# Converting w_out on one engine, pairing tiles f and f+8, and making the first operands of the last product earlier, in an attention + MoE kernel

## The chip, the cores and the metric

The kernel runs on one core of a Trainium2 chip. The metric is the device time of one execution in microseconds, the median of three runs. The names of the engines are those of the profile: PE (TensorE), DVE (VectorE), ACT (ScalarE), POOL (GpSimd), and SP, whose queue issues nearly all DMA transfers here. Each engine runs its own instructions strictly in the order of the program.

## The reference

```python
attn_out = softmax(q k^T / 8 + bias) v        # 4 batches, 8 heads, 576 positions, 64 wide
x = attn_out as 2304 tokens x 512
h = x @ w_in                                  # 512 -> 2048
g = h * tanh(softplus(h))                     # Mish
out = g @ w_out                               # 2048 -> 512, all float32
```

## The kernel before

The attention takes about the first 290 us of the span, and nothing of it is changed. What follows is the MoE part, over four blocks of tokens (512, 768, 512, 512). Every float32 operand of a product is split into a rounded part "hi" and a rest "lo" (ACT makes hi with a copy that rounds, DVE makes lo with a subtraction), and the product is the sum hi·hi + lo·hi + hi·lo.

**Blocks 0, 2 and 3** (`hidden` and `gate`): for each of the 16 tiles f of 128 columns of w_in, `hidden` puts 12 matmuls into one of four PSUM buffers h, and `gate` lets ACT write Mish of h into a buffer g. Tiles f and f+8 share one g buffer; after the second of the two, POOL adds one half of it to another (L692) and SP writes the whole to HBM (L693, `g_d`). The order of the tiles is `FORDER`: 0 to 3, then 8 to 11, then the rest in pairs. Since PE has four buffers h, it can be at most four tiles ahead of ACT. **Block 1** (`product`, `gates`) does the same in a form with seven products (a Strassen scheme).

**Beside blocks 2 and 3** three more things run. (1) w_out arrives as 64-bit words in 16 pieces; `load_weights` (L107) fetches each into one of three buffers, and `conv_weights` turns it into float32 with four instructions: a multiplication (L129 on ACT, or L131 on DVE), and L134, L136, L138 on DVE. One call of `convert` issues one step of that, and four calls finish a piece. (2) `split_x` turns the x of the next block into hi and lo: a multiplication (L653, DVE), a copy (L654, ACT) and a subtraction (L656, DVE). (3) `combine(m)` makes the seven right-hand operands of the last product from w_out (a subtraction L897 or L903 on DVE, two copies L900 on ACT, two subtractions L901 on DVE).

**The last product** (out = g @ w_out) runs over nine token tiles p with seven products each (`multiply(p, m, t)`, t = 0 for the hi of g, 1 for its lo). `load_g(p)` reads g back from HBM, `prepare(p, m)` makes the left-hand operand m in one of four buffers gslot: ACT copies (L927), DVE subtracts (L928). `prepare(p, 2)` first subtracts on DVE (L924), and afterwards lets POOL make two more sums, L930 and L931, in its own queue. `leave` takes results out of PSUM: `leave(0, 0)` copies the first product on ACT to `p1s` (in the tile `la`, L966), and PE may add product 2 into the same PSUM bank only after that.

The ring `rt` holds, one behind the other, x of block 3, the g buffers, and later combo6 and three of the gslot buffers: a gslot that lies where a g buffer was can be written only when that buffer's transfer to HBM has ended. In the kernel before gslot2 lies on g buffers 0 and 1, gslot3 on 2 and 3.

Of the kernel before, what the change touches and what calls it, by code (L numbers as in the profile page):

```python
# [7 lines left out]
F32 = mybir.dt.float32  # L8
F32R = mybir.dt.float32r
# [7 lines left out]
HP = H // 2  # L17
DM, DFF = 512, 2048
NT = B * S
P = 128  # L20
# [10 lines left out]
TB = 512  # L31
# [15 lines left out]
def kernel(ctx: ExitStack, tc, qk, v, wb, w2, w_in, w_out, psia, psi4, rinv, eye, out):  # L47
# [378 lines left out]
    def convert(on_act, last):  # L426
        if not conv and w64 and last not in done:
            done.append(w64[0][0])
            conv.append(conv_weights(on_act))
        elif conv and next(conv[0]):  # L430
            conv.clear()
            load_weights()
            if w32 and w32[0][0] in order[:EARLY]:
                split_weights(pool)
# [82 lines left out]
    bps_t, h_t = {}, {}  # L517
# [14 lines left out]
    for idx, t in enumerate(ts):  # L532
        spent["a"] += 0.75 + (1.9 if idx in SOFT_AT else 0.0)
        spent["v"] += (1.6 if idx in SOFT_AT else 0.0)
        n = reach(t)[2]
# [58 lines left out]
    for idx in range(NB + 2):  # L594
# [16 lines left out]
        if idx - 2 in SOFT_AT[1:]:  # L611
            f = s_ps.tile([P, 2, 512], F32, name="s")
# [18 lines left out]
    rt = sbuf("rt", 1, side="right").ring(11 * 4096)  # L631
# [6 lines left out]
    xc = []  # L638
    g_bufs = []

    XPARTS = [(x, d) for x in "hl" for d in range(HP)]

    def begin_x(blk, raw, hl):
        load_x(blk, raw)
# [3 lines left out]
    def split_x(blk, parts):  # L648
        n = blocks[blk][1]
        for x, d in parts:  # L650
            raw, hi, lo = (y[blk][:, d, :n] for y in (x_raw, x_hi, x_lo))
            if x == "h":
                dve.tensor_tensor(raw, raw, lo.bitcast(F32), op=ALU.mult)  # L653
                act.copy(hi, raw)  # L654
            else:
                dve.tensor_tensor(lo, raw, hi.bitcast(F32), op=ALU.subtract)  # L656


    FORDER = [0, 1, 2, 3, 8, 9, 10, 11, 4, 12, 5, 13, 6, 14, 7, 15]
    units = {blk: [(blk, i, (f,)) for i, f in enumerate(FORDER)] for blk in (0, 2, 3)}  # L660
    h_t, g_t, n_g = {}, {}, [4]

    def w_at(f, d):
        return [x[:, f % 4] for x in w_split["i", f // 4, d]]
# [12 lines left out]
    def gate(blk, i, fs):  # L677
        n = blocks[blk][1]
        j = fs[0] % 8
        if (blk, j) not in g_t:  # L680
            if blk == 0:
                g_t[blk, j] = g_own[j]
            else:
                g_t[blk, j] = g_bufs[n_g[0] % 5]
                n_g[0] += 1
        g = g_t[blk, j]
        c0 = fs[0] // 8 * n
        act.activation(g[:, c0:c0 + len(fs) * n], h_t.pop((blk, fs)), AF.Mish)  # L688
        if fs[-1] >= 8:
            del g_t[blk, j]  # L690
            g = g.rearrange("p (k t) -> p k t", k=4)
            pool.tensor_tensor(g[:, 1], g[:, 1], g[:, 3], op=ALU.add)  # L692
            sp.dma_start(out=g_d[blk][:, :, j].rearrange("k p t -> p k t"), in_=g)  # L693
# [157 lines left out]
    x2_hl = [xa_t[:, t].bitcast(F32R) for t in range(2)]  # L851
    AT_STEP = {(0, 0): ((x1_lo, 5),), (0, 3): ((x1_hi, 6),), (0, 4): ((x1_lo, 6),), (0, 6): ((begin_x, 2, x2, x2_hl),)}
    for n, part in enumerate(XPARTS):
        AT_STEP[divmod(11 + n, 7)] = ((split_x, 2, (part,)),)
    for p in range(4):
        for k in range(7):
            product(p, k)
# [10 lines left out]

    xp_raw = rt.tile([P, HP, TB], F32, name="xraw")
    xp_hl = [rt.tile([P, HP, TB], F32R, name=name) for name in ("xhi", "xlo")]  # L870
    g_bufs += [rt.tile([P, 2 * TB], F32, name="g") for _ in range(5)]

    q_t.append(ring.tile([P, 4, 8, 256], F32, name="quarters"))
    b11, b12, b21, b22 = (q_t[0][:, q] for q in range(4))
# [13 lines left out]
    slots = [ring.tile([P, 2, 8, P], F32R, name="gslot1")]  # L888
# [6 lines left out]
    def combine(m):  # L895
        if m in w_sum:
            dve.tensor_tensor(w_src[m], *w_sum[m], op=ALU.subtract)  # L897
        for half in (slice(0, 4), slice(4, 8)):
            hi, lo = wc[m][:, half, 0:256], wc[m][:, half, 256:512]
            act.copy(hi, w_src[m][:, half])  # L900
            dve.tensor_tensor(lo, w_src[m][:, half], hi.bitcast(F32), op=ALU.subtract)  # L901
        if m == 2:
            dve.tensor_tensor(b11, b21, b11, op=ALU.subtract)  # L903
# [89 lines left out]

    def reuse_x():
        wc[6] = rt.tile([P, 8, 512], F32R, name="combo6")
        slots.extend(rt.tile([P, 2, 8, P], F32R, name=f"gslot{k}") for k in (2, 3))

    for blk in (2, 3):
        for i in range(16):
            if blk == 2:  # L1000
                if i == 2:
                    begin_x(3, xp_raw, xp_hl)
                if 6 <= i < 14:
                    split_x(3, XPARTS[i - 6:i - 5])
            hidden(*units[blk][i])
            if (2, 0) < (blk, i) <= (3, 0):
                for _ in range(4):
                    convert(True, None)
            if blk == 3:
                if i == 0:  # L1010
                    combine(0)
                    slots.insert(0, rt.tile([P, 2, 8, P], F32R, name="gslot0"))
                elif i == 2:
                    combine(1)
                elif i == 5:
                    combine(2)
                elif i == 8:
                    load_g(0)
                elif i == 9:
                    combine(3)  # L1020
                elif i == 11:
                    prepare(0, 0)
                elif i == 13:
                    combine(4)
                elif i == 14:
                    prepare(0, 1)
                elif i == 15:
                    reuse_x()
                    prepare(0, 2)
            gate(*units[blk][i])  # L1030
    load_g(1)
    prepare(0, 3)
    combine(5)
# [95 lines left out]
```

## Time and profile before

| | |
|---|---|
| median of three runs | 651.92 us (651.9 to 652.0) |
| profiled execution: its own time | 651.97 us |
| profiled execution: span from first to last instruction | 650.2 us |
| PE busy | 633.4 us, 97% of the span |
| DVE busy | 486.5 us, 75% |
| ACT busy | 427.8 us, 66% |
| POOL busy | 174.3 us, 27% |

The profile shows one execution. Busy time counts instructions at work; an engine whose share is far below 100% can still be the one that others wait for over a stretch of some microseconds. Times in the views are microseconds from the first instruction.

### The profile page before, as it was taken

To read this page: it belongs to the slowest core of one execution; us is meant where nothing else is said; L and a number is where in the kernel's file an instruction comes from. 1 tells how busy PE (TensorE), PEld (TensorE's weight loads), DVE (VectorE), ACT (ScalarE), POOL (GpSimd) and SP (SyncE) were. 2 spreads that over 40 slices of the span, in tenths; PEclk is the share of its full clock that TensorE was granted. 3 is DMA by queue.
4 is the path that set the end of the run, shared out by engine and by line. 5 is a ranking of instruction groups with operands and counts; after the bars stand their busy time and mean duration, and the time that the engine had idled before them with its cause. 6 is when DMAs were issued, how large, how long until landed. Compare 5 with 4: busy or idle time off the path is not lost.

```text
span 650.2 us, 14512 instructions
## 1 busy us (share of the span) xinstructions
PE 633.4 (97%) x5504; PEld 500.6 (77%) x5504; DVE 486.5 (75%) x919; ACT 427.8 (66%) x886; POOL 174.3 (27%) x150
## 2 busy tenths in 40 slices
PE   6989999999999999999999999999999999999997
PEld 2436677777777777778899998877888888888886
DVE  7995888988888888635646535888698777777875
ACT  6886899989999999854566643446475434455432
POOL 0000133333222334405253511114243221122220
PEclk9999999999999999999999999999999999999999
DMA  8986486677758766029236369862846545433401
GB/s 275 297 275 205 142 266 211 234 234 240 261 187 270 256 189 181 23 62 281 97 132 198 126 222 289 280 213 83 273 134 191 162 146 163 145 109 96 152 17 50
DMA packets 99622, 119.71 MB, mean 184 GB/s; under 512 B 15200, under 2 KB 75616, under 8 KB 99552
## 3 DMA queue, kind: packets, MB, share of 16 engines
q1 hardware_dynamic: 97248, 110.59, 53.0%
q0 software_dynamic: 1872, 8.09, 4.2%
q8 instruction: 44, 0.72, 0.4%
q14 instruction: 26, 0.21, 0.1%
q10 hardware_dynamic: 432, 0.09, 0.1%
HBM read 79.47 MB, written 39.28 MB: 183 GB/s over the span
## 4 chain that ended last, share of the span: by engine, by line
PE 75%; DVE 9%; DMA 6%; ACT 5%; issue 4%; SPq 1%; POOL 0%; DVEq 0%; ACTq 0%
PE h L673 11%; PE s L232 10%; PE o L356 10%; PE y L949 8%; PE h L949 8%; PE bps L601 6%; PE tp L318 4%; PE h L953 4%; PE y L953 4%; PE y L790 3%; PE h L790 3%; DMA w<-in_w_out_dram 2%; DVE pt L249 2%; PE te L301 2%; PE o L360 1%
## 5 line engine op out<-in xcount | busy, mean ns | idle before, releaser
L264 ACT ACTIVATE pt<-pt,m 128x576 f32<-128x576 f32 x144 | 112.0, 787 | 2.7 <-DVE m L249 2.2
L249 DVE CUSTOM_DVE_ANT_0 pt<-s,bias 128x576 f32<-128x576 f32 (+1 forms) x112 | 81.6, 754 | 22.8 <-PE s L232 17.2
L183 POOL TENSOR_TENSOR qklo<-rawqk,qkhi 128x304 fp32r<-128x304 f32 x52 | 46.7, 923 | 118.9 <-DMA rawqk<-in_qk_dram 109.6
L356 PE MATMUL o<-main,vt 128*64 128x256 f32 (+1 forms) x512 | 76.1, 418 | 0.0
L326 ACT COPY main<-tp 128x512 f32<-128x512 f32 x126 | 68.2, 599 | 0.9 <-DMA bias_d<-bt 0.9
L232 PE MATMUL s<-qkhi 64*128 64x288 f32 x260 | 57.0, 341 | 0.9
L318 PEld LDWEIGHTS tp<-ident,pt 64*128 64x128 f32 x1184 | 54.8, 138 | 2.0 <-ACT main L326 0.5
L318 PE MATMUL tp<-ident,pt 64*128 64x64 f32 x1184 | 56.0, 222 | 0.2 <-ACT main L326 0.2
L927 ACT CAST gslot<-graw 128x1024 fp32r<-128x1024 f32 x30 | 31.2, 1052 | 36.3 <-DVE graw L924 28.0
L692 POOL TENSOR_TENSOR g<-g 128x256 f32<-128x256 f32 x24 | 27.3, 1143 | 95.7 <-ACT g L688 81.7
L601 PE MATMUL bps<-ht,w2t 128*32 128x79 f32 (+49 forms) x640 | 42.9, 403 | 8.9 <-ACT ht L551 6.3
L927 ACT CAST gslot<-quarters 128x1024 fp32r<-128x1024 f32 x28 | 29.1, 1055 | 32.4 <-DVE quarters L924 26.0
L928 DVE TENSOR_TENSOR gslot<-graw,gslot 128x1024 fp32r<-128x1024 f32 x30 | 41.9, 1433 | 10.6 <-ACT gslot L927 10.6
L232 PE MATMUL s<-qklo,qkhi 64*128 64x288 f32 x260 | 48.0, 297 | 0.0
L232 PE MATMUL s<-qkhi,qklo 64*128 64x288 f32 x260 | 46.4, 291 | 0.0
L356 PEld LDWEIGHTS o<-main,vt 128*64 128x64 f32 x512 | 31.8, 136 | 17.2 <-ACT tail L332 0.4
L673 PE MATMUL h<-xa,lc 128*128 128x512 f32 x192 | 43.8, 389 | 0.0
L601 PEld LDWEIGHTS bps<-ht,w2t 128*32 128x32 f32 x640 | 17.2, 113 | 34.4 <-ACT bt L581 14.9
L928 DVE TENSOR_TENSOR gslot<-quarters,gslot 128x1024 fp32r<-128x1024 f32 x28 | 39.5, 1454 | 5.0 <-ACT gslot L927 5.0
L553 DVE TENSOR_SCALAR ht<-at,bb 128x560 f32<-128x560 f32 (+17 forms) x120 | 43.2, 440 | 0.0
L673 PEld LDWEIGHTS h<-xa,lc 128*128 128x128 f32 x192 | 36.0, 188 | 7.5
L688 ACT ACTIVATE g<-h 128x512 f32<-128x512 f32 x48 | 28.0, 593 | 20.1 <-PE h L673 16.9
(206 smaller groups left out, 1498.7 us busy)
## 6 DMA issues: line engine op xcount, KB each, us to landing
g_d<-g SPq DMA_DIRECT2D x24, 512.0 KB
bias_d<-bt SPq DMA_DIRECT2D x36, 295.5 KB
w<-in_w_in_dram SPq DMA_DIRECT2D x16, 512.0 KB
w<-in_w_out_dram SPq DMA_DIRECT2D x16, 512.0 KB
quarters<-g_d SPq DMA_DIRECT2D x16, 512.0 KB
qkhi<-in_qk_dram POOLq DMA_DIRECT2D x13, 608.0 KB, 5.1
rawqk<-in_qk_dram SPq DMA_DIRECT2D x13, 608.0 KB
graw<-g_d SPq DMA_DIRECT2D x15, 512.0 KB
```

Of the source, the lines that this page charges most:

```text
L232: pe.matmul(s[:, j, :SH], q[rows, c * P:(c + 1) * P], k[rows, KO + j * SH:KO + (j + 1) * SH], start=(t == 0), stop=(t == len(terms) - 1))
L249: dve.tensor_tensor_reduce(out=halves(pt[rows, sl]), in0=s[rows, :, :SH], in1=halves(bt[rows, sl]), scale=-0.125, scalar=BIG, op0=ALU.add, ...
L264: act.activation(ps, ps, AF.Exp, bias=m[:, u:u + 1], scale=-1.0, accum_out=sums[i][:, k:k + 1])
L318: pe.transpose(tp[:, k * 64:k * 64 + 64], pt[rows, c0:c0 + P], ident[rows, rows])
L326: copy(main[:, :, :, q0:q0 + 64], tp.rearrange("p (h k q) -> p h k q", h=2, k=4))
L356: pe.matmul(o[h * 64:h * 64 + 64, :w], vt[:, h, k, :], main[:, h, k, :], start=(k == 0), stop=False, **kw)
L601: pe.matmul(ps[cg * 32:cg * 32 + 32, a:a + n], w2t, h_t[idx, cg][:, cols], start=True, stop=True)
L673: pe.matmul(h[:, u * n:(u + 1) * n], w_at(f, d)[t], x[:, d, :n], start=(k == 0), stop=(k == 11))
L927: act.copy(hi, src)
L928: dve.tensor_tensor(lo, src, hi.bitcast(F32), op=ALU.subtract)
L949: pe.matmul(o, x[:, f], wc[m][:, f], start=(f == 0 and m in (0, 1, 3)), stop=(f == 7), **kw)
L953: pe.matmul(o[:, 0:256], x[:, f], wc[m][:, f, 0:256], start=False, stop=(f == 7), **kw)
```

## The change

Four things are changed. The multiplication of each w_out piece moves from ACT (L129) to DVE (L131), and three calls of `convert` follow each tile instead of four, so that the 16 pieces end at tile 6 of block 3 instead of tile 0. The tiles of blocks 2 and 3 come in the order 0, 8, 1, 9, ... (`PAIRED`), with three g buffers instead of five. The parts of `split_x` are ordered so that DVE multiplies one step ahead of ACT's copy. And the operands of the last product are placed anew: gslot2 gets room of its own at tile 0 of block 3, gslot3 now lies on g buffers 0 and 1 (those of pairs 5 and 6 of block 3), `load_g(0)` comes one tile earlier, `prepare(0, 1)` and `prepare(0, 2)` come at tiles 12 and 13 instead of 14 and 15, and `combine(2)` and `combine(4)` come later. Line numbers shift by 1 to 4 (L692 becomes L695, L924 L927, L927 L930, L930 L933, L931 L934, L966 L969).

```diff
-    XPARTS = [(x, d) for x in "hl" for d in range(HP)]
+    XPARTS = [[("m", 0)]] + [[("h", d), ("m", d + 1)] for d in range(HP - 1)] + [[("h", HP - 1), ("l", 0)]]
+    XPARTS += [[("l", d)] for d in range(1, HP)]
...
-            if x == "h":
+            if x == "m":
                 dve.tensor_tensor(raw, raw, lo.bitcast(F32), op=ALU.mult)
+            elif x == "h":
                 act.copy(hi, raw)
...
-    units = {blk: [(blk, i, (f,)) for i, f in enumerate(FORDER)] for blk in (0, 2, 3)}
-    h_t, g_t, n_g = {}, {}, [4]
+    PAIRED = [f for j in range(8) for f in (j, j + 8)]
+    units = {blk: [(blk, i, (f,)) for i, f in enumerate(PAIRED if blk else FORDER)] for blk in (0, 2, 3)}
+    h_t, g_t, n_g = {}, {}, [2]
...
-                g_t[blk, j] = g_bufs[n_g[0] % 5]
+                g_t[blk, j] = g_bufs[n_g[0] % 3]
...
-    g_bufs += [rt.tile([P, 2 * TB], F32, name="g") for _ in range(5)]
+    g_bufs += [rt.tile([P, 2 * TB], F32, name="g") for _ in range(3)]
...
-        slots.extend(rt.tile([P, 2, 8, P], F32R, name=f"gslot{k}") for k in (2, 3))
+        slots.append(rt.tile([P, 2, 8, P], F32R, name="gslot3"))
...
-            if (2, 0) < (blk, i) <= (3, 0):
-                for _ in range(4):
-                    convert(True, None)
+            if (2, 0) < (blk, i) <= (3, 6):
+                for _ in range(3):
+                    convert(False, None)
             if blk == 3:
                 if i == 0:
                     combine(0)
+                    g2 = rt.tile([P, 2, 8, P], F32R, name="gslot2")
                     slots.insert(0, rt.tile([P, 2, 8, P], F32R, name="gslot0"))
+                    slots.append(g2)
                 elif i == 2:
                     combine(1)
-                elif i == 5:
+                elif i == 7:
                     combine(2)
-                elif i == 8:
                     load_g(0)
                 elif i == 9:
                     combine(3)
                 elif i == 11:
                     prepare(0, 0)
+                elif i == 12:
+                    prepare(0, 1)
                 elif i == 13:
+                    prepare(0, 2)
+                elif i == 14:
                     combine(4)
-                elif i == 14:
-                    prepare(0, 1)
-                elif i == 15:
-                    reuse_x()
-                    prepare(0, 2)
             gate(*units[blk][i])
+    reuse_x()
     load_g(1)
     prepare(0, 3)
     combine(5)
```

On POOL, at the end of block 3, the queue before held 15 of the 16 additions on g ahead of the two sums of `prepare(0, 2)` (each g_ number is one use of a buffer; graw and la hold g read back):

```order
L692 TENSOR_TENSOR g_6281<-g_6281 128x256
L930 TENSOR_TENSOR graw_6790<-la_5459,graw_6789 128x1024
L931 TENSOR_TENSOR graw_6789<-graw_6791,graw_6789 128x1024
L692 TENSOR_TENSOR g_6282<-g_6282 128x256
L930 TENSOR_TENSOR quarters_6283<-quarters_6283 128x1024
```

The same place in the queue of the changed kernel:

```order
L695 TENSOR_TENSOR g_6278<-g_6278 128x256
L933 TENSOR_TENSOR graw_6773<-la_5459,graw_6772 128x1024
L934 TENSOR_TENSOR graw_6772<-graw_6774,graw_6772 128x1024
L695 TENSOR_TENSOR g_6279<-g_6279 128x256
L695 TENSOR_TENSOR g_6280<-g_6280 128x256
L933 TENSOR_TENSOR quarters_6281<-quarters_6281 128x1024
```

The additions of pairs 6 and 7 (g_6279 and g_6280) now stand behind both sums; g_6279 is g buffer 1, on which gslot3 lies.

On ACT, at the same place, the changed kernel issues the following (L691 is a gate, L903 a copy of `combine`, L930 of `prepare`, L969 `leave(0, 0)`):

```order
L691 ACTIVATE g_6279<-h_6848 128x512
L930 CAST gslot2_6635<-graw_6772 128x1024
L691 ACTIVATE g_6279<-h_6864 128x512
L903 CAST lc_5461<-quarters_6281 128x4x256 x2
L691 ACTIVATE g_6280<-h_6885 128x512
L691 ACTIVATE g_6280<-h_6904 128x512
L930 CAST gslot3_6921<-graw_6774 128x1024
L903 CAST lc_5461<-quarters_6281 128x4x256 x2
L969 COPY la_5459<-y_6932 128x512
```

The copy to `la` that releases PE's third product stands behind the copy into gslot3, as it did before; the gates no longer lie between the copies of the first three slots as they did.

On DVE, the stretch from the last w_out pieces to the subtraction of `prepare(0, 2)` reads now:

```order
L904 TENSOR_TENSOR lb<-quarters,lb 128x4x256 x2
L931 TENSOR_TENSOR gslot_6636<-graw,gslot_6636 128x1024
L931 TENSOR_TENSOR gslot_6283<-graw,gslot_6283 128x1024
L927 TENSOR_TENSOR graw<-graw 128x1024
L931 TENSOR_TENSOR gslot_6635<-graw,gslot_6635 128x1024
L900 TENSOR_TENSOR quarters<-quarters 128x2048
L904 TENSOR_TENSOR lc<-quarters,lc 128x4x256 x2
L931 TENSOR_TENSOR gslot_6921<-graw,gslot_6921 128x1024
```

The long subtraction of `combine(4)` (L900) now follows the operands of `prepare(0, 2)`, where before it came ahead of the second operand.

## Rows read from the trace of the kernel before

**Rows 1.** Windows: stretch; busy PE, PEld, DVE, ACT, POOL; clock; DMA share; GB/s.

```profile
381.40:424.98 43.58, 43.58 (x194) 36.06 (x193) 27.16 (x42) 17.65 (x32) 5.98 (x7) 1.00 0.90 294
424.98:470.69 45.71, 44.16 (x194) 35.88 (x192) 34.96 (x32) 23.31 (x34) 13.66 (x9) 1.00 0.54 180
490.00:647.00 157.00, 156.71 (x905) 138.68 (x903) 120.16 (x108) 71.03 (x87) 38.93 (x16) 1.00 0.38 121
```

**Rows 2.** Timeline of PE: start, time, line, tiles, count, idle before and its releaser.

```profile
356.32 1.34 PE L790 MATMUL y<-xcombo,wsums 128*128 128x384 f32 x6 [0.17 <-ACT gs L803]
...
437.15 2.14 PE L673 MATMUL h<-xhi,lb 128*128 128x512 f32 x8 [1.13 <-ACT g L688]
...
443.35 2.12 PE L673 MATMUL h<-xhi,lb 128*128 128x512 f32 x8 [0.42 <-ACT g L688]
...
470.69 1.98 PE L949 MATMUL y<-combo,gslot 128*128 128x512 f32 x8
...
476.25 1.22 PE L953 MATMUL y<-wearly,gslot 128*128 128x256 f32 x8
...
488.06 2.06 PE L949 MATMUL y<-combo,gslot 128*128 128x512 f32 x8 [0.42 <-DVE quarters L974]
```

**Rows 3.** Timeline of ACT around the first two of these waits.

```profile
434.03 0.69 ACT L129 ACTIVATE quarters<-w 128x512 f32<-128x512 f32 x1 [2.60 <-DMA w<-in_w_out_dram]
...
440.81 2.00 ACT L900 CAST xa<-quarters 128x1024 fp32r<-128x1024 f32 x2 [3.22 <-DVE quarters L897]
```

**Rows 4.** The tile w: durations in ns as min/median/max, first and last start.

```profile
L134 DVE TENSOR_SCALAR w<-w x16: 416/421/980, 387.2 to 434.0; 128x512 uint32<-128x512 uint32 x16
L136 DVE SCALAR_TENSOR_TENSOR quarters<-quarters,w x16: 691/693/696, 387.7 to 434.8; 128x512 uint32<-128x512 uint32 x16
L138 DVE SCALAR_TENSOR_TENSOR quarters<-w,quarters x16: 691/693/1119, 388.4 to 435.5; 128x512 uint32<-128x512 uint32 x16
...
L131 DVE TENSOR_SCALAR wraw<-w x13: 384/423/1229, 68.9 to 233.2; 128x512 f32<-128x512 f32 x13
```

**Rows 5.** Timelines of SP and ACT: loads of block 3's x, and a piece behind them.

```profile
385.83 0.56 SPq L376 DMA_DIRECT2D xraw<-x_d  x1
...
398.47 0.69 ACT L129 ACTIVATE quarters<-w 128x512 f32<-128x512 f32 x1 [5.33 <-DMA w<-in_w_out_dram]
```

**Rows 6.** Timeline of DVE: one of each other kind of its instructions in blocks 2 and 3.

```profile
414.01 0.68 DVE L653 TENSOR_TENSOR xraw<-xraw,xlo 128x512 f32<-128x512 f32 x1
...
438.48 2.29 DVE L897 TENSOR_TENSOR quarters<-quarters 128x2048 f32<-128x2048 f32 x1
441.89 2.36 DVE L901 TENSOR_TENSOR xa<-quarters,xa 128x1024 fp32r<-128x1024 f32 x2 [1.12 <-ACT xa L900]
...
470.04 1.21 DVE L924 TENSOR_TENSOR graw<-graw 128x1024 f32<-128x1024 f32 x1
472.42 3.60 DVE L928 TENSOR_TENSOR gslot<-graw,gslot 128x1024 fp32r<-128x1024 f32 x2 [1.16 <-ACT gslot L927]
```

**Rows 7.** Timeline of POOL at the end of block 3.

```profile
431.57 0.76 POOL L692 TENSOR_TENSOR g<-g 128x256 f32<-128x256 f32 x1 [4.64 <-ACT g L688]
...
471.39 2.41 POOL L930 TENSOR_TENSOR graw<-la,graw 128x1024 f32<-128x1024 f32 x1 [2.35 <-DVE graw L924]
475.02 3.27 POOL L931 TENSOR_TENSOR graw<-graw 128x1024 f32<-128x1024 f32 x1 [1.21 <-DVE gslot L928]
478.25 1.72 POOL L692 TENSOR_TENSOR g<-g 128x256 f32<-128x256 f32 x1
```

**Rows 8.** The chain that ended last, 467 to 478: start, time, what.

```profile
469.07 2.75 DMA g_d<-g
```

**Rows 9.** Timeline of ACT where the last product begins.

```profile
472.78 1.04 ACT L927 CAST gslot<-graw 128x1024 fp32r<-128x1024 f32 x1
```

**Rows 10.** Groups of PE by shape, from 6 to 10.2 us: busy, mean ns, idle before.

```profile
L601 PE MATMUL bps<-ht,w2t 128*32 128x497 f32 x8 | 2.0, 1033 | 0.0
...
L601 PE MATMUL bps<-ht,w2t 128*32 128x15 f32 x8 | 0.8, 224 | 6.4 <-ACT ht L551 6.3
```

**Rows 11.** The same from 10.4 to 16 us.

```profile
L601 PE MATMUL bps<-ht,w2t 128*32 128x496 f32 x8 | 1.0, 580 | 0.0
```

More of the change, by code (lines that the diff above doesn't have):

```diff
@@ L853 @@
     for n, part in enumerate(XPARTS):
-        AT_STEP[divmod(11 + n, 7)] = ((split_x, 2, (part,)),)
+        AT_STEP[divmod(11 + n, 7)] = ((split_x, 2, part),)
     for p in range(4):
@@ L1003 @@
                 if 6 <= i < 14:
-                    split_x(3, XPARTS[i - 6:i - 5])
+                    split_x(3, XPARTS[i - 6])
             hidden(*units[blk][i])
-            if (2, 0) < (blk, i) <= (3, 0):
-                for _ in range(4):
-                    convert(True, None)
+            if (2, 0) < (blk, i) <= (3, 6):
+                for _ in range(3):
+                    convert(False, None)
             if blk == 3:
```

## The prediction

> **What bounds the kernel now.** I read the windows view first, by stage [rows 1]. In block 2 PE is busy for 43.58 of 43.58 us, so a tile of `hidden` costs 43.58 / 16 = 2.72 us and nothing can be gained there. Block 3 holds the same 16 tiles and takes 45.71 us: 2.13 us are lost. From 490 us on PE is idle for 0.3 us in 157. So PE is the bound, and all that an edit of the other engines can win after the attention is the few places where PE waits.
>
> The timeline of PE names them [rows 2]: 0.17 us in block 1 (on an ACT copy), 1.13 and 0.42 us in block 3 (on gates, both on ACT), and 0.42 us at the end of the first tile of the last product (on DVE). The two waits of block 3 show 1.55 us and cost 2.13, so each restart of PE costs about 0.29 us more than the row shows. With that the four are worth 0.46 + 2.13 + 0.71 = 3.30 us. This is the most that the change can win.
>
> Why do the gates come late? The timeline of ACT shows it [rows 3]: ACT stands for 2.60 us before a multiplication of a w_out piece that has not landed, and for 3.22 us before a copy of `combine(1)` that needs DVE's subtraction. The gates queue behind both.
>
> **The change, part by part.** (1) *x split*: DVE's multiplication comes one step ahead of ACT's copy. In block 1 ACT no longer stands before the copy with other work behind it; DVE's order there is the same. I give it the whole 0.46 us. Were ACT late all the same, these 0.46 us would be missing.
>
> (2) *w_out on DVE*: ACT no longer waits for a landing, so the 1.13 us wait goes. DVE takes L131 for each piece: 0.42 + 0.42 + 0.69 + 0.69 = 2.23 us a piece [rows 4]. At three calls a tile, that is 0.75 pieces or 1.67 us in 2.72 us: it fits, but what DVE has beside it counts too. I lay DVE's queue end to end, from the third piece to the subtraction of `prepare(0, 2)` (L927 after the change). The start: before, the piece behind the loads of x started at 398.47, with the loads issued from 385.83 [rows 5]; now these loads stand in SP's queue behind the first write of g, which POOL can release only after tile 1 (381.40 + 2 x 2.72, then a gate and an addition, about 389), up to 3.3 us later. I take 401. The work: 14 pieces, 31.2; eight parts of x at 0.60 to 0.68, 4.8; four pairs of `combine` at 2.36 and three long subtractions at 2.29, 16.3; three instructions of 1.21 for the operands, 3.6; two waits of 1.12 for ACT's first copy [rows 6]; and POOL's additions. An addition of 0.76 us [rows 7] holds DVE up: L138 takes 0.69 us by the median and 1.12 at most [rows 4], so 0.42 each, times 11 additions, 4.6. In sum 31.2 + 4.8 + 16.3 + 3.6 + 2.2 + 4.6 = 62.7, so L927 ends at 463.7. From below: it cannot end before tile 11 of block 3 (424.98 + 12 x 2.72 = 457.6), one copy of 1.04 us [rows 9] and two DVE instructions of 1.21, so 461. From above: were the loads held up the full 3.3 us, so that DVE starts at 401.8, and the pieces behind them as much as 1.5 us later still, L927 would end at 466. I take 463.7, because this sum leaves DVE without a pause for 60 us, and nothing speaks for a pause.
>
> With the same sum `combine(1)`'s subtraction ends at about 438, its copies take 2 us on ACT, and the gate behind them is done at 440.7; PE wants that buffer at 424.98 + 6 x 2.72 = 441.3. The 0.42 us wait of block 3 goes too, with 0.6 us to spare. If this margin fails, the loss is hidden by what follows, because part 4 is late by the clock and not by PE.
>
> (3) *Pairs and three g buffers*: a buffer is wanted again six tiles (16 us) after its first use, and a write takes 2.75 us [rows 8]; this costs nothing in block 2. What hides it is that distance; with one buffer it would stall each pair.
>
> (4) *First operands sooner*. This is the part on which the result rests. After `prepare(0, 2)` POOL has its two sums, L933 and L934, and only then the additions of pairs 6 and 7. Before, only the last addition stood there, and nobody waited for it. Now gslot3 lies on the g buffer of pair 6. So the copy into gslot3 on ACT waits for pair 6's write, this for its addition, this for both sums; behind the copy on ACT stand the two copies of `combine(5)` and the copy to `la` (L969), and PE's third product waits for that one.
>
> How long is this chain? The rows of before show it in the same order, one pair later. DVE's L924 ends at 470.04 + 1.21 = 471.25 [rows 6]; then POOL's 2.41, an L928 on DVE that has to wait for it, a second L928, POOL's second sum (3.27 with its wait), one of DVE's L901, and the addition (1.72 with its wait), which ends at 478.25 + 1.72 = 479.97 [rows 7]. The two engines take turns: the pair of L928 takes 3.60 us and not 2.4 [rows 6]. The chain is 8.7 us long. In the changed order the second L928 is replaced by the L900 of `combine(4)`, 2.29 us instead of 1.21: 9.8 us. From below, were the engines not to hold each other up, it would be 2.41 + 2.3 + 0.7 = 5.4 us. I take 9.8, because the order is the same as in the rows.
>
> So pair 6's addition ends at 463.7 + 9.8 = 473.5, its write 2.75 us later [rows 8], at 476.3. Before, PE's third product began at 476.25 and the copy into gslot3 at 472.78 [rows 2, 9], that is 3.47 us earlier, with the same instructions between. So PE starts the third product at 479.8. It could start at 468.56 (424.98 + 43.58, no waits) plus the 5.56 us between 470.69 and 476.25 [rows 2], so at 474.1. PE waits for 5.7 us.
>
> **The sum.** At the third product PE is late against before by 479.8 + 0.29 - 476.25 = +3.84 us. The 0.71 us at the end of the first tile go (DVE has half of that stretch's work behind it, and PE comes later): -0.71. Block 1: -0.46, which moves all of this together. Net +2.67 us on 651.97 us, the profiled execution's own time (its span and 1.8 us around it), so 654.6; the median of the runs is 0.05 us lower, and I say 654.6.
>
> **PE's clock.** The rows at the start of the kernel show what PE does after it has stood idle: after 6.3 us without work, 128x497 matmuls take 2.0 us for eight until 10.2 us [rows 10], and from 10.4 us on 128x496 take 1.0 us for eight [rows 11]. [...]
>
> **Rivals.** *A, the wait without the clock*: 654.6, as worked out. *B, the wait and then half the clock*: 654.6 + 2 = 656.6; the start of the kernel speaks for it [rows 10], but PE comes from rest there and not from work. *C, the chain is short enough*, the case on the other side: if L927 ended at 461 and POOL and DVE did not hold each other up, the write would land at 461 + 5.4 + 2.75 = 469.2, PE would start at 472.6 or earlier, which is before 474.1, and all 3.30 us would be won: 648.7. It decides at a landing of 474.1 - 3.47 = 470.6. Against it speak the rows that show the two engines in turns [rows 6, 7]. *D, DVE is not late but the chain is long*: 461 + 9.8 + 2.75 + 3.47 = 477.0, plus 0.29, is 1.05 us later than before, less 1.17: 651.9, no change. For it speaks only that my sum for DVE has 60 us of terms.
>
> **Numbers.** A change of under 0.2% (1.3 us) can hardly be told from none. A 0.42, B 0.34, C 0.10, D and what lies around it 0.14. A alone reaches from 653.3 to 656. A and B give slower 0.76 plus 0.01 of D; C and a little of D give faster 0.11; same 0.12. The range goes from D's 651.9 to a B in which DVE is 1 us later still, 657.6: left out are C, part of D and the far end of B, together some 0.2.
>
> **What would show it.** In the profile of the changed kernel: no idle before the tiles of block 3, and the product starting near 468; in PE's timeline one wait of 4 to 7 us at the third product (`wearly`), released by ACT's copy to `la`; on ACT a wait before the copy into gslot3, released by a write of g; on POOL the additions of pairs 6 and 7 behind both sums; L131 on DVE 16 times more, and DVE busy without a gap from 401 on. The clock of the 20 us after that wait tells A from B. I would be wrong if gslot3's copy finds the write done, or if DVE reaches L927 much before 463.

## The result, and the profile after

The changed kernel takes 656.88 us by the median of six runs (656.56 to 658.55); the kernel before took 651.96 us beside it. The ratio is 1.0081, with a 95% interval from 1.0067 to 1.0095: 0.8% slower, 4.9 us. The profiled execution took 658.55 us, the longest of the six; its span is 656.8 us. Single executions far above all others (775.31 us for the kernel before, here) are left out of the ratios, while the medians count them.

The timeline of PE in the changed kernel (start, time, line, tiles, count, idle before and its releaser) has these waits after the attention, and behind them the products that follow the longest one:

```profile
360.86 1.34 PE L793 MATMUL y<-xcombo,wsums 128*128 128x384 f32 x6 [0.38 <-ACT u2a L810]
365.82 1.34 PE L793 MATMUL y<-xcombo,lc 128*128 128x384 f32 x6 [0.50 <-DVE gs L816]
...
443.11 2.11 PE L676 MATMUL h<-xhi,wearly 128*128 128x512 f32 x8 [0.47 <-ACT g L691]
...
470.45 1.98 PE L952 MATMUL y<-combo,gslot 128*128 128x512 f32 x8
...
482.06 2.08 PE L956 MATMUL y<-wearly,gslot 128*128 128x256 f32 x8 [5.91 <-ACT la L969]
483.93 2.60 PE L952 MATMUL y<-wearly,gslot 128*128 128x512 f32 x8
486.37 2.00 PE L952 MATMUL y<-lb,gslot 128*128 128x512 f32 x8
488.21 1.98 PE L952 MATMUL y<-lc,gslot 128*128 128x512 f32 x8
```

Three things are to be seen against [rows 2]. The waits of 1.13, 0.42 and 0.42 us are gone, and a smaller one (0.47 us) has come in block 3. PE stands 5.91 us before its third product, released by ACT's copy to `la`. And the eight 128x256 matmuls behind this wait take 483.93 - 482.06 = 1.87 us until the next product starts, where before they took 477.31 - 476.25 = 1.06 us. From the third product to the one on `lc` it is 6.15 us now and was 4.71 us (476.25 to 480.96). The rows of before that this is read from, behind 476.25 in [rows 2]:

```profile
477.31 2.00 PE L949 MATMUL y<-wearly,gslot 128*128 128x512 f32 x8
...
480.96 1.98 PE L949 MATMUL y<-lc,gslot 128*128 128x512 f32 x8
```

The windows view around the wait (stretch; busy PE, PEld, DVE, ACT, POOL; granted clock; DMA share; GB/s) says why:

```profile
477.00:478.00 1.00, 0.00 (x0) 0.00 (x0) 0.00 (x0) 0.00 (x0) 0.31 (x1) 1.00 1.05 372
478.00:479.00 1.00, 0.00 (x0) 0.00 (x0) 0.00 (x0) 0.42 (x1) 0.00 (x0) 0.69 0.80 281
479.00:485.00 6.00, 2.94 (x11) 2.75 (x12) 5.22 (x5) 5.38 (x7) 0.00 (x0) 0.50 1.09 305
485.00:486.00 1.00, 1.00 (x5) 0.77 (x5) 0.64 (x1) 0.00 (x0) 0.00 (x0) 0.90 1.15 348
486.00:490.00 4.00, 4.00 (x19) 3.30 (x18) 1.86 (x2) 3.43 (x5) 0.00 (x0) 1.00 0.85 249
```

PE's last matmul ends at 476.15 (482.06 - 5.91); between 478 and 479 the granted clock falls from 1.00 to 0.50 (a mean of 0.69 there, 0.50 from 479 to 485), and it comes back between 485 and 486 (a mean of 0.90 there, so early in it), some 3 us after PE has begun again at 482.06.

The chain that ended last, from 463 to 483 (start, time, what), shows what the 5.91 us consist of:

```profile
464.75 1.15 DVE graw L927
...
467.00 2.51 DVE gslot L931
...
469.64 0.10 POOL graw L934
469.74 4.19 issue
473.93 1.73 POOL g L695
...
475.67 2.75 DMA g_d<-g
...
478.58 1.04 ACT gslot L930
479.63 1.89 ACT lc L903 x2
481.52 0.49 ACT la L969
```

This is part (4) of the forecast, link by link: L927, the two sums with DVE between them (the 4.19 us called issue are the rest of the second sum, which takes 4.33 us in POOL's timeline), pair 6's addition, its write, the copy into gslot3, `combine(5)`'s copies, the copy to `la`. L927 starts late because DVE starts its third w_out piece late; the timelines of SP and of DVE show it:

```profile
389.72 0.38 SPq L696 DMA_DIRECT2D g_d<-g  x1
390.14 0.56 SPq L376 DMA_DIRECT2D xraw<-x_d  x1
...
393.77 1.56 SPq L107 DMA_DIRECT2D w<-in_w_out_dram  x2
```

```profile
404.32 0.43 DVE L131 TENSOR_SCALAR quarters<-w 128x512 f32<-128x512 f32 x1 [11.23 <-DMA w<-in_w_out_dram]
```

SP issues the loads of x only behind the first write of g, 4.3 us later than before, and the next w_out loads behind them: the third piece is there 5.85 us later than in [rows 5], and 4.67 us when the later start of block 2 (1.18 us) is taken off.

From the starts of the same matmuls in both profiles, the difference of the spans (656.8 - 650.2 = 6.6 us) divides up as follows, beside the forecast's terms for the same stretches:

| Stretch of PE | before, us | after, us | difference | forecast |
|---|---|---|---|---|
| to the start of block 2 | 381.42 | 382.60 | +1.18 | -0.46 |
| block 2 | 43.56 | 43.56 | 0.00 | 0 |
| block 3 | 45.71 | 44.29 | -1.42 | -2.13 |
| last product, start to third product | 5.56 | 11.61 | +6.05 | +5.97 |
| third product to the one on `lc` | 4.71 | 6.15 | +1.44 | 0 (A), 2 (B) |
| the rest | 169.24 | 168.59 | -0.65 | -0.71 |

### The profile page after: what moved, and what is told of

Same layout as the page of the kernel before. It is cut to its first block, busy times and chain, and to the rows that moved or that the text cites. A ratio compares the mean times of both kernels' runs of the same rounds, so it can differ in the third digit from the quotient of the medians.

```text
span 656.8 us, 14501 instructions
## 1 busy us (share of the span) xinstructions
PE 635.1 (97%) x5504; PEld 502.1 (76%) x5504; DVE 492.8 (75%) x935; ACT 418.4 (64%) x870; POOL 172.0 (26%) x150
## 4 chain that ended last, share of the span: by engine, by line
PE 75%; DVE 11%; DMA 6%; issue 4%; ACT 3%; POOL 0%; SPq 0%; DVEq 0%; ACTq 0%; POOLq 0%
PE s L232 11%; PE o L356 11%; PE y L952 9%; PE h L952 8%; PE h L676 8%; PE bps L601 6%; PE tp L318 5%; PE y L956 5%; PE h L956 4%; PE y L793 3%; PE h L793 3%; PE te L301 2%; DVE pt L249 2%; DVE quarters L138 1%; PE o L360 1%
## 5 line engine op out<-in xcount | busy, mean ns | idle before, releaser
L930 ACT CAST gslot<-graw 128x1024 fp32r<-128x1024 f32 x30 | 31.2, 1052 | 38.5 <-DVE graw L927 30.7
L691 ACT ACTIVATE g<-h 128x512 f32<-128x512 f32 x48 | 27.9, 596 | 37.3 <-PE h L676 33.6
L930 ACT CAST gslot<-quarters 128x1024 fp32r<-128x1024 f32 x28 | 29.0, 1055 | 30.3 <-DVE quarters L927 27.3
L931 DVE TENSOR_TENSOR gslot<-graw,gslot 128x1024 fp32r<-128x1024 f32 x30 | 41.5, 1418 | 9.0 <-ACT gslot L930 8.8
L695 POOL TENSOR_TENSOR g<-g 128x256 f32<-128x256 f32 x24 | 24.2, 1012 | 91.7 <-ACT g L691 85.4
L931 DVE TENSOR_TENSOR gslot<-quarters,gslot 128x1024 fp32r<-128x1024 f32 x28 | 37.5, 1385 | 4.8 <-ACT gslot L930 4.8
```

The source lines that it names most:

```text
L930: act.copy(hi, src)
L931: dve.tensor_tensor(lo, src, hi.bitcast(F32), op=ALU.subtract)
```

## The experiments

Each time stands against the kernel before on the same chip; other chips spread more than the first did (before: 651.96 to 652.67 us by the median). The ratio is to the kernel before, with its 95% interval.

### The chain to the third product

**sums_late: the two POOL sums (L933 and L934, taken out of `prepare(0, 2)` as `sums`) behind the last gate**

```diff
             gate(*units[blk][i])
+    sums(0)
     reuse_x()
```

> The changed kernel with one thing moved: the two POOL sums of prepare(0, 2) come behind the last gate, so that the additions of pairs 6 and 7 no longer stand behind them. Theory 1 (the chain sums, addition, write of pair 6, copy into gslot3, copy to la makes PE wait 5.9 us, and the clock falls behind it): the write lands near 471, the copy into gslot3 follows the gates at about 474.7, the copy to la ends at 478.2, PE waits about 2.2 us for its third product, and the clock falls little or not at all: 651.5 to 652.5 us. Theory 2 (the copy is held by ACT's and DVE's own order, combine(4) above all, and the write only happens to end last): wait above 4.5 us, over 655. Theory 3 (much of the loss comes from block 1 and not from this place): as theory 1 in the trace, but the time stays above 653.5.

652.67 us, ratio 1.0009 (0.9998 to 1.0020). PE's timeline has 1.20 us in place of 5.91, and a new wait two products on:

```profile
475.74 1.22 PE L960 MATMUL y<-wearly,gslot 128*128 128x256 f32 x8 [1.20 <-ACT la L973]
...
481.75 2.11 PE L956 MATMUL y<-lc,gslot 128*128 128x512 f32 x8 [1.14 <-ACT la L977]
```

The order of three instructions in POOL's queue thus decides about 4 us. The clock stays at 1.00. Theory 1 stands, though the wait is 1.20 us where it had 2.2 and the time lies just above its range; part of what it wins goes to the operand of the product on `lc`, which needs the sums and now comes later.

**leave_first: `prepare(0, 3)` and `combine(5)` behind `leave(0, 0)`**

```diff
-    prepare(0, 3)
-    combine(5)
     for p in range(len(tiles)):
...
         leave(p, 0)
         if p:
             multiply(p - 1, 6, 1)
             leave(p - 1, 6)
-            prepare(p, 3)
+        prepare(p, 3)
+        if p == 0:
+            combine(5)
```

> The changed kernel with one thing moved: prepare(0, 3) and combine(5) come behind leave(0, 0), so that on ACT the copy to la no longer stands behind the copy into gslot3; pair 6's write is as late as before (lands near 478.5). Theory 1: no wait at the third product; then about 0.8 us for the product that reads gslot3 and about 1 us for the next one, whose operand ACT copies behind combine(5); clock at 1.00 throughout; 651 to 652.5 us. Theory 2 (PE wants gslot3 and what stands behind it as urgently as la, so the wait only moves one product on): a wait of 4 us or more at the product that reads gslot3, over 654.

655.23 us, ratio 1.0043 (1.0028 to 1.0059). The third product doesn't wait; PE's timeline has two waits behind it:

```profile
479.83 2.14 PE L952 MATMUL y<-lb,gslot 128*128 128x512 f32 x8 [0.74 <-ACT gslot L930]
484.59 2.09 PE L952 MATMUL y<-lc,gslot 128*128 128x512 f32 x8 [2.62 <-ACT la L973]
```

More than theory 1 had (0.8 and 1), less than theory 2 (4 or more). ACT's order carries the late write one or two products on, but in the profiled execution the granted clock stays at 1.00 through a wait of 2.62 us. The time is theory 2's (over 654). Four of the six executions have a mean granted clock of 0.996 or 0.997 over the whole span, as those of the changed kernel have (0.994 to 0.997), and the profiled one has 1.00; so the clock most likely fell in those four as well, though no trace shows where.

**both_moved: both at once**

> Both moves at once: the sums behind the last gate, and prepare(0, 3) and combine(5) behind leave(0, 0). Theory 1: neither the write nor ACT's order holds PE, no wait above 0.5 us between 467 and 490, clock 1.00: 656.9 - 5.9 - 1.4 = 649.6 us, below the kernel before. Theory 3 (block 1 holds part of the loss): 651 or more with no wait at the last product's start.

652.76 us, ratio 1.0004 (0.9993 to 1.0015): a miss by 3 us. The first two waits are gone, and others are left: 0.35 us in block 1, 0.29 in block 3, 0.79 at the end of the first tile, and 1.62 at the product on `lc`. That one is the price of the late sums: ACT stands 0.72 us before the copy that takes the second sum, and the copy to `la` that releases the product stands behind it.

**xload_first: the loads of block 3's x one tile sooner**

```diff
-                if i == 2:
+                if i == 1:
                     begin_x(3, xp_raw, xp_hl)
```

> The changed kernel with the loads of block 3's x issued one tile sooner, so that they stand ahead of the first write of g on SP (before the change they did). Theory: these loads go out near 386 instead of 389 to 390, the pieces behind them land 3 to 4 us sooner (DVE starts the third near 400 instead of 402 to 404.5), DVE ends L927 as much sooner, and with it the addition and the write of pair 6; PE's wait at the third product falls from 5.9 to 2 - 3 us: 652.5 to 654 us. Rival (the chain is set by the write or by ACT, or other loads delay the pieces): the wait stays above 4.5 us, over 655.

655.67 us, ratio 1.0049 (1.0032 to 1.0066). The third piece starts at 398.83 us on DVE and L927 at 460.63 instead of 464.67. PE's wait is 3.79 us:

```profile
478.01 1.75 PE L956 MATMUL y<-wearly,gslot 128*128 128x256 f32 x8 [3.79 <-ACT la L969]
479.56 3.06 PE L952 MATMUL y<-wearly,gslot 128*128 128x512 f32 x8
```

The wait and the time miss the theory's ranges (2 to 3 us, 652.5 to 654 us); the time is the rival's (over 655). So the order of the loads on SP is one link, worth some 2 us of the wait, and not the whole: L927 now ends at 461.84, close to the earliest that the forecast allowed (461), and the chain behind it is still long enough to make PE wait. The clock still fell, to 0.50 between 480 and 481 us: 1.58 us more than at full clock from here to the product on `lc` (6.27 against 4.69).

**late_ops: `combine(4)`, `prepare(0, 1)`, `prepare(0, 2)` back at tiles 13, 14, 15**

```diff
-                elif i == 12:
-                    prepare(0, 1)
-                elif i == 13:
-                    prepare(0, 2)
-                elif i == 14:
+                elif i == 13:
                     combine(4)
+                elif i == 14:
+                    prepare(0, 1)
+                elif i == 15:
+                    prepare(0, 2)
```

> The changed kernel with combine(4), prepare(0, 1) and prepare(0, 2) back at tiles 13, 14 and 15; pairs, three g buffers and the places in memory stay changed. The sums on POOL then stand behind the addition of pair 6, but DVE reaches L927 some 5 us later (combine(4) ahead of it). Theory 1: pair 6's write lands before 471, the copy into gslot3 doesn't wait for it; PE waits for the third product's own operand, 1 to 2.5 us, and the clock falls for less than 1 us or not at all: 651.5 to 653.5 us. Theory 2 (the early operands are not what costs, but pairs and three buffers): over 655 us.

651.88 us, ratio 0.9981 (0.9968 to 0.9995), with 0.93 us at the third product and the clock at 1.00 there. Pairs, three buffers and the new places in memory cost little that shows (x_conv below, which leaves them out, is 1.0 us lower by the medians on the same chip, and the intervals overlap); the early operands are the edit that makes the kernel slower.

### The price of the clock

**keep_busy: the wait filled with 24 matmuls**

```diff
         multiply(p, 1, 1)
+        if p == 0:
+            spare = y_ps.tile([P, TB], F32, name="y")
+            for k in range(24):
+                pe.matmul(spare, slots[1][:, 0, k % 8], wc[1][:, k % 8], start=(k == 0), stop=(k == 23),
+                          skip_group_check=True)
         leave(p, 1)
```

> The changed kernel with 24 extra matmuls (128x512, some 5.4 us) in front of the third product, which write a PSUM buffer that nobody reads; they fill the wait of 5.9 us. Theory B (the clock falls in the wait and its return costs time): granted clock 1.00 there, and the time falls by 1.4 to 2.0 us, to 655 - 655.5. Theory A (the wait alone costs): 656.6 to 657, unchanged. If the wait in the unprofiled runs were shorter than 5.4 us, the matmuls would add to it and the time would rise above 657.

656.41 us, ratio 1.0068 (1.0050 to 1.0085). The third product starts 11.61 us behind the start of the last product, as in the changed kernel; from it to the product on `lc` it is 4.69 us instead of 6.15, at a clock of 1.00. The trace says 1.46 us. The time misses theory B's 655 to 655.5 us: it came from another chip than the changed kernel's, and the intervals overlap. So the next pair stands on one chip.

**after_same and keep_busy26: the changed kernel, and 26 matmuls in its wait, on one chip**

> The changed kernel once more, beside the next one on the same chip, so that the price of the clock can be read as a difference of times. 656 to 658 us, a wait of 5.5 to 6 us at the third product, and the granted clock at 0.5 from about 2.3 us into it until about 3.8 us behind it.

> The changed kernel with 26 extra matmuls (128x512, 5.9 us) in front of the third product, two more than in the earlier run, so that next to nothing of the wait is left idle. Theory B: the traces show from the start of the third product to that of the product on lc 6.15 us with the clock at half and 4.69 us at full clock, so the time is 1.46 us below the changed kernel on the same chip (1.0 to 1.9 with the spread). Theory A (the clock's fall costs nothing in time): equal within 0.5 us.

658.59 us, ratio 1.0094 (1.0066 to 1.0122), and 656.65 us, ratio 1.0056 (1.0034 to 1.0079): the filled wait is 1.94 us faster by the medians. The intervals of the ratios overlap at their ends (1.0066 to 1.0079), but each of the five executions of the changed kernel (657.71 us and more) is longer than each of seven with the wait filled (657.45 us and less; an eighth, at 885.14 us, lies far above all others). The timeline of PE, first of the changed kernel, then with the 26 matmuls:

```profile
481.46 2.08 PE L956 MATMUL y<-wearly,gslot 128*128 128x256 f32 x8 [5.93 <-ACT la L969]
483.34 3.20 PE L952 MATMUL y<-wearly,gslot 128*128 128x512 f32 x8
486.37 1.98 PE L952 MATMUL y<-lb,gslot 128*128 128x512 f32 x8
488.18 1.98 PE L952 MATMUL y<-lc,gslot 128*128 128x512 f32 x8
```

```profile
476.20 6.08 PE L1054 MATMUL y<-xa,gslot 128*128 128x512 f32 x26
482.29 1.21 PE L956 MATMUL y<-wearly,gslot 128*128 128x256 f32 x8
483.33 2.00 PE L952 MATMUL y<-wearly,gslot 128*128 128x512 f32 x8
485.17 1.98 PE L952 MATMUL y<-lb,gslot 128*128 128x512 f32 x8
486.98 1.98 PE L952 MATMUL y<-lc,gslot 128*128 128x512 f32 x8
```

Both reach the third product 11.6 us behind the start of the last product. From there to `lc` it is 6.72 us with the wait empty and 4.69 with it filled: 2.03 us, as the medians say. Case B is shown.

### The parts by themselves

**x_only: the kernel before with part (1)**

> The kernel before with part (1) alone: the new order of the parts of the x split. The forecast's step: ACT's copies no longer hold block 1, 0.46 us faster than the kernel before on the same chip. The rival, read from the changed kernel's trace: ACT's gates, no longer held, release POOL's additions about 1.1 us sooner, these fall on DVE's second multiplication (1.5 us instead of 0.69), and PE waits 0.35 to 0.5 us near 365 us for DVE: the same time as before to 0.5 us slower.

649.68 us, ratio 0.9952 (0.9929 to 0.9975): 3 us faster. Both theories miss. PE has one wait left (0.51 us in block 1, for DVE, as the rival had it), and none in block 3. Where the 3 us come from is to be seen beside block 2. The kernel before, timelines of ACT and of DVE:

```profile
404.09 0.62 ACT L654 CAST xhi<-xraw 128x512 fp32r<-128x512 f32 x1 [3.26 <-DVE xraw L653]
404.62 0.65 ACT L129 ACTIVATE quarters<-w 128x512 f32<-128x512 f32 x1
```

```profile
403.38 0.69 DVE L653 TENSOR_TENSOR xraw<-xraw,xlo 128x512 f32<-128x512 f32 x1
403.98 0.42 DVE L134 TENSOR_SCALAR w<-w 128x512 uint32<-128x512 uint32 x1
405.31 0.70 DVE L136 SCALAR_TENSOR_TENSOR quarters<-quarters,w 128x512 uint32<-128x512 uint32 x1 [0.91 <-ACT quarters L129]
```

And DVE at the same place with part (1):

```profile
404.00 0.68 DVE L654 TENSOR_TENSOR xraw<-xraw,xlo 128x512 f32<-128x512 f32 x1
404.60 0.42 DVE L134 TENSOR_SCALAR w<-w 128x512 uint32<-128x512 uint32 x1
405.12 0.69 DVE L136 SCALAR_TENSOR_TENSOR quarters<-quarters,w 128x512 uint32<-128x512 uint32 x1
```

The two engines wait in a ring: ACT's copy of x waits for DVE's multiplication, ACT's multiplication of w_out stands behind that copy, and DVE's L136 waits 0.91 us for it, in four tiles (405.31 to 415.94), 3.64 us in all. With the multiplication one tile ahead the ring is open: the first `combine` starts on DVE at 432.78 us instead of 436.09, and the `combine` instructions behind it are 3.3 us sooner as well.

**x_block1 and x_block2: part (1) for one block's x only**

> The kernel before with the new order of the x split for block 2's x alone (the part that runs beside block 1). By the forecast's step: 0.46 us faster. By the traces so far (POOL's additions come 1.1 us sooner and fall on DVE's second multiplication; PE then waits 0.5 us for DVE instead of 0.2 to 1.4 us for ACT, depending on when x lands): between 0.5 us faster and 0.5 us slower, and block 3 keeps its waits of about 1.1 and 0.4 us.

> The kernel before with the new order of the x split for block 3's x alone (the part that runs beside block 2). Theory from the run with part (1) alone: in the kernel before DVE stands 0.91 us in four tiles for ACT's multiplication of w_out, which stands behind ACT's copy of x, which waits for DVE; the new order opens this ring, the last pieces are ready 3.3 us sooner, and the waits of block 3 and of the last product go: 2.5 to 3.1 us faster than the kernel before. Rival (part (1) won in block 1 or by the chip's own spread): less than 1 us.

Beside block 1 alone: 652.73 us, ratio 1.0013 (1.0001 to 1.0025); block 3 keeps its waits of 1.13 and 0.45 us. Beside block 2 alone: 649.34 us, ratio 0.9957 (0.9940 to 0.9973), with a single wait of PE after the attention, 0.33 us in block 1. The gain beside block 2 is what the forecast had priced for its two waits of block 3 and the one at the end of the first tile together, 2.13 + 0.71 = 2.84 us. The whole gain of part (1) comes from block 2; in block 1, where the forecast had it, there is a small loss. DVE's timeline in x_block1 shows a multiplication of x that took 0.69 us in the kernel before and takes 1.50 now (x_only, with the same order beside block 1, has 1.50 us for it from 353.06 on, with POOL's additions from 352.77 to 355.44):

```profile
353.94 1.50 DVE L655 TENSOR_TENSOR la<-la,xa 128x512 f32<-128x512 f32 x1
```

**conv_only: the kernel before with part (2)** (and `combine(2)` at tile 7, where the last piece is ready)

> The kernel before with part (2) alone: w_out multiplied by DVE, three calls a tile up to tile 6 of block 3, and combine(2) at tile 7, because it needs the last piece; tiles, g buffers and operands of the last product as before. The forecast's step: the waits of 1.13 and 0.42 us of block 3 go, and nothing else: 1.5 to 2.1 us faster than the kernel before. The rival: DVE, with 13 more multiplications and a third piece that is now loaded behind x, is late for the operands of the last product, which stand at the same tiles as before: block 3 runs without a wait and the product's third step waits longer, the same time or up to 3 us slower.

650.67 us, ratio 0.9972 (0.9959 to 0.9986). No wait in block 3, 0.42 us left at the end of the first tile, and 1.41 us in block 1, where x landed late in this execution. As the forecast's step had it.

**x_conv: parts (1) and (2)**

> The kernel before with parts (1) and (2) together. Theory: both take away the same waits of block 3, so the second wins nothing more: 2 to 3 us faster than the kernel before, as part (1) alone, and no wait of PE between 381 and 640 us above 0.5 us. Rival (the two add up): 4.5 us or more faster. Against the changed kernel it shows the price of parts (3) and (4): 6 to 7 us.

650.87 us, ratio 0.9976 (0.9963 to 0.9988). The two don't add up: both free the same waits of block 3. Against the changed kernel (1.0081, on another chip) parts (3) and (4) cost 0.0105 of the time, 6.8 us, as was expected.

### Put together

**best1 and best2: all parts, with the places found so far mended.** Both take the loads of x one tile sooner, the sums directly behind pair 6's addition and `leave_first`'s order; best1 has the old order of the x split, best2 the new one beside block 2 only.

> The changed kernel with four things: the loads of x one tile sooner, the x split in its old order, the two POOL sums directly behind the addition of pair 6 (so between the additions of pairs 6 and 7), and prepare(0, 3) and combine(5) behind leave(0, 0). If the places found so far are all there is: no wait of PE above 0.5 us between 425 and 500, 648.5 to 650 us, faster than both kernels. If DVE, busy without a gap, is late once more for products 3 to 5: 650.5 to 652.

> The changed kernel with the loads of x one tile sooner, the new order of the x split beside block 2 only, the two POOL sums directly behind the addition of pair 6, and prepare(0, 3) and combine(5) behind leave(0, 0). If nothing else of parts (2) to (4) costs: no wait of PE above 0.5 us from 381 us on, 648.5 to 649.5 us, as the kernel before with the new x order beside block 2 (649.3 on another chip). If DVE is late for products 3 to 5 as in the earlier combination (0.81 us wait): 650 to 651.

650.65 us, ratio 0.9973 (0.9962 to 0.9984), and 650.78 us, ratio 0.9973 (0.9959 to 0.9988). Both beat the kernel before, and neither has a wait in block 3 or at the third product; both times are those of the second case. What is left in PE's timeline of best2 behind the attention is 0.38 us in block 1 and this:

```profile
479.73 2.11 PE L957 MATMUL y<-lc,gslot 128*128 128x512 f32 x8 [0.81 <-ACT la L978]
```

ACT's copy of the third result stands behind a copy into a slot (478.15 to 479.10 us in its timeline) that it has no need of. Parts (2) to (4), freed of the chain, win nothing over part (1) beside block 2, which has the lowest time of all (649.34; x_only's 649.68 can't be told from it).

## Why the prediction was right in direction and short in size

**The mechanism of part (4) was right.** The wait was forecast at 5.7 us behind L927, the sums, pair 6's addition and its write; it is 5.91, and the third product comes 11.61 us behind the start of the last product where the working had 11.53. The links are later than forecast by the clock: L927 ends at 465.88 instead of 463.7, the write lands at 478.4 instead of 476.3. DVE's third piece was taken to start at 401 and starts at 404.32: 1.18 us of that are the later start of block 2, the rest are the loads behind the first write of g. From there to the end of L927 DVE needs 61.56 us where the working laid 62.7, which takes 1.1 us back. sums_late and late_ops show that the order is the cause: 4 us or more come back.

**The step that failed is the choice of A over B**: the sum put the clock behind the wait at nothing. A (the wait costs only itself) had 0.42, B (half the clock on top) 0.34, with the argument that PE comes "from rest there and not from work". It made no difference: the clock fell behind matmuls at a granted clock of 1.00 as well. B's term of 2 us was the author's estimate from [rows 10, 11], and no run shows it as a fixed price; in its place the runs show 1.44 us (the profiled execution), 1.58 (xload_first) and 2.03 (after_same), and with the wait filled the time falls by 1.94. B's 656.6 us stands beside a measured 656.88, but in part by luck: its sum has the terms of block 1 that failed (below), and its price comes from a stretch in which the trace reads a granted clock of 1.00 (6 to 10.2 us), so that it is open whether the rate halved there by the clock. In the wait the fall is in the rows: a granted clock of 1.00 between 477 and 478 us, 0.69 between 478 and 479, and 0.50 from 479 to 485.

**Part (1) was mis-sized, in both its places.** In block 1, -0.46 us was forecast; x_block1 measures 0.13% more, about 0.8 us (0.01 to 0.25%), and block 2 starts 1.18 us later in the profiled execution of the changed kernel. The step held that DVE's order is the same there, which is right, but ACT's gates, no longer held, release POOL's additions sooner (at 352.07 us in sums_late, where x landed as in the kernel before, which has 354.29), and these fall on DVE's work. In sums_late two of POOL's additions run from 352.07 to 354.74 us, and DVE's multiplication of x that starts at 352.35 takes 1.51 us; before, the same one starts at 352.44, ahead of POOL's additions, and takes 0.69. That POOL's additions lengthen it is read from these times; what holds DVE up was not shown.

Most of the 1.18 us is something else. DVE's first multiplication of x waits for a transfer (for one that lands x in 15 of the 17 traces; the rows of the other two, that of after among them, name a write of g); it stands ahead of all that the new order moves, and starts between 350.18 and 351.96 us. DVE's timeline, before and after:

```profile
350.31 0.69 DVE L653 TENSOR_TENSOR la<-la,xa 128x512 f32<-128x512 f32 x1 [1.28 <-DMA xa<-r_d]
```

```profile
351.32 0.69 DVE L654 TENSOR_TENSOR la<-la,xa 128x512 f32<-128x512 f32 x1 [2.50 <-DMA g_d<-gs]
```

From this start to that of block 2 it is 31.11 us before (350.31 to 381.42) and 31.28 us after (351.32 to 382.60); the five traces with the old order beside block 1 have 31.09 to 31.11, the twelve with the new one 31.26 to 31.31. So the new order costs 0.17 us here, and 1.01 us of the 1.18 are the later transfer, which comes in either order (351.96 us in conv_only, with the old one). That the profiled execution lies 1.7 us above the median may be this transfer too; the other executions have no trace.

In block 2 the step gave part (1) nothing, and it is worth 2.8 us there. [rows 6] has DVE's instructions but not its four waits of 0.91 us for ACT; the forecast went by the waits of PE alone and put ACT's lateness down to landings that were late [rows 3], where a ring of the two engines had put off the whole queue.

**Part (2)** was right in size by itself: conv_only wins 2.0 us where 2.13 was forecast. But ACT's wait for a landing was not the whole reason, since x_only, in which ACT still multiplies, has no wait in block 3 either. In the changed kernel block 3 keeps 0.47 us, since the pieces start later (xload_first, where they start sooner, has no wait there); so the forecast's margin of 0.6 us there failed, at no cost, because PE then waits for the chain anyhow. **Part (3)** costs nothing, as forecast (block 2 takes 43.56 us in both).

**The sum.** 2.67 us were forecast, and the spans differ by 6.6. Block 1 adds 1.64 (0.46 that didn't come, 0.17 lost, 1.01 of the later transfer), block 3 and the wait together 0.79 (4.63 in place of 3.84), the clock 1.44, the rest 0.06. Without the transfer, which differs from execution to execution, it is 5.6 us, against 4.9 measured on one chip and 6.2 on the other.

## What to carry to other kernels

Before an operand is made sooner, list for every queue what it is put ahead of, and what lies in the memory that is written next: here three POOL instructions in another order cost some 4 us. A long wait of TensorE has to be priced with the clock behind it: the waits of 3.79 to 5.93 us in these traces cost 1.4 to 2.0 us more than themselves. And where two engines hand each other work in every tile, read the waits of both, also of those that PE never waits for by name: opening four waits of 0.91 us on DVE won 2.8 us here, and all of the rest of this change won nothing on top of it.

## What was not expected of the hardware

The clock can fall after PE is back at work. In xload_first PE stood from 474.2 to 478.01 us. The windows view of that kernel:

```profile
477.00:478.00 1.00, 0.00 (x0) 0.00 (x0) 1.00 (x2) 1.00 (x3) 0.00 (x0) 1.00 1.14 344
478.00:480.00 2.00, 1.99 (x10) 1.89 (x11) 2.00 (x2) 2.00 (x3) 0.00 (x0) 0.61 1.15 347
480.00:481.00 1.00, 1.00 (x4) 0.81 (x3) 0.87 (x2) 0.34 (x1) 0.00 (x0) 0.50 1.16 341
481.00:482.00 1.00, 1.00 (x4) 0.77 (x3) 0.60 (x1) 0.00 (x0) 0.00 (x0) 0.58 1.15 346
```

The granted clock is 1.00 up to the restart and 0.50 behind it; it is at 1.00 again from 482. In the two traces of the changed kernel it falls within the wait instead (a mean of 0.69 between 478 and 479 in the first, of 0.53 between 479 and 480 in after_same). What it cost beyond the wait was 1.44, 1.58 and 2.03 us in the three traces, with waits of 5.91, 3.79 and 5.93 us, so the length of the wait does not order the losses. The return does: worked out from the granted clock of the microsecond in which it comes back (0.90, 0.58 and 0.55), full clock is there about 3.1, 3.8 and 4.4 us behind PE's restart.

The traces with waits of 1.20 and 2.62 us show a granted clock of 1.00 throughout, but that is one execution each: four other executions of leave_first, whose trace has the 2.62 us, have a lower mean clock, and so do single executions of the kernel before (0.995 in one of 656.87 us). Where PE waited in those, nothing on record shows.
